# The left-over rows' output product in a forward recurrence: summed over all heads per 128 output columns, and turned by VectorE in 32x32 blocks

## The chip, the core and the metric

The kernel runs on one core of a Trainium2 chip. The metric is the device time of one execution in microseconds (us), lower is better. TensorE multiplies (PE in the profile; its weight loads, which overlap the multiplications, are PEld), VectorE (DVE), ScalarE (ACT) and GpSimd (POOL) do the rest, and SyncE (SP) issues transfers.

## What is computed

The reference is a forward and backward pass of a parallel sum: a memory-augmented recurrent attention (A) and a squared-ReLU feed-forward layer (B), with gradients of the input, the first memory and all weights. The change lies in the forward pass of A:

```python
for s in range(n_seg):                       # 64 segments of 32 rows
    xs = x[:, s * seg_len:(s + 1) * seg_len, :].copy()
    h = jnp.concatenate([mem, xs], axis=1)   # 8 memory rows, then 32 rows
    q = jnp.einsum('btd,dhe->bhte', h, Wq)   # 32 heads of 128, d = 512
    ...
    p = _softmax(scores, axis=-1)
    o = jnp.einsum('bhqk,bhke->bhqe', p, v)
    o = jnp.einsum('bhte,hed->btd', o, Wo)
    mem = o[:, :M, :].copy()                 # the next segment's memory
    outs.append(o[:, M:, :])
```

Only the first 8 rows of `o` feed the next segment. Nothing waits for the rest inside the recurrence.

## The kernel before

The kernel works in stages: layer norm and B (to some 305 us), the forward recurrence (305 to 1203), a stage that prepares the backward pass (1222 to 1455), the backward recurrence (1455 to 2415) and the weight gradients (2470 to the end). The change is in the forward recurrence.

A segment has 40 query rows. The 32 rows that are done at once (8 memory rows and 24 others) are a *step*, `fwd(s)`. The 8 left over are put aside and done later, for four segments together, as 32 rows: that is `left(b)`, for a block b of four segments. There are 64 steps and 16 blocks. The heads are laid out as 4 groups (HG, index g) of 8 (KH, index k), and TensorE is used as four column groups of 32, so that four matmuls with 32 stationary columns each run side by side, the one of group c writing PSUM partitions 32c to 32c+31 (`tile_position=(0, 32 * g)`).

The order of all work is written out by hand. `F_ORDER` (L603) has four strings, one for each step of a block (j = 0 to 3); names without a prefix are operations of the step, names with `L.` are operations of a left-over block, and a `+` or `-` behind a name moves it one round later or earlier. `play` (L581) issues the operations in that order, and every engine works through its own share in order. `ENGS` (L620) says which engine does a copy (`L.ra` and `ra` VectorE, `rb` ScalarE). The left-over block played beside block n is n - 1.

A step's chain is: K, Q and V projections (`k0mm` to `v1mm`, L392), evictions to SBUF, turns of K and Q (`k0fl` and so on, evicted by `k0Te` and so on), scores (`s0`, `s1`, L437), softmax on VectorE and ScalarE (`mx`, `sb`, `ex`, `su`, `rc`, `pm`), a turn of E on VectorE (`tu`, L450), the products with V (`w0`, `w1`, L547) and their evictions (`oa`, `ob`, to OT), the output product over all heads (`g0`, `g1`, L460), its copy to SBUF (`ra`, `rb`), four fp32 turns on TensorE (`ta`, `tb`, L469), and VectorE's sum over the four head groups, of the memory rows into X (`HT`, L482), which is the next step's input, and of the other rows into XT (`xt`).

The left-over block does the same for its 32 rows: `L.S0` to `L.W1`, evictions to OTL, and then the part that changes:

- `L.G0` and `L.G1` (`gather`, L453 to 462): the output product, one half each (p = 0, 1; in the order written, G1 comes first, in the third step, and G0 in the fourth). For each k, four matmuls, one per head group g in column group g, with 32 columns of OTL as weights and the head's whole `Wo[:, h, :]` of 512 columns moving. So PSUM's ps_RL holds four partial sums, one per head group, of 32 rows by 512 columns.
- `L.ra`: VectorE copies ps_RL (128x512 fp32) to SBUF, R4L.
- `L.ta`, `L.tb` (`turn_ops`, L464): TensorE turns R4L in four fp32 blocks of 128x128 into a further PSUM buffer, ps_sum.
- `L.xt` (`left_sums`, L473): VectorE sums the four head groups out of ps_sum, in four reductions, into the rows 0 to 7 of each segment of XT (128 x 4 x 4 x 32 fp32, two buffers).

`L.BT` in the next block's first step turns XT back to rows (`block_rows`, L485), `L.out` adds and `L.sx` stores them. PSUM buffers of the stage are four banks of one kind ("r"), shared by all of these, and the pair of bank pairs f_pp for `w`.

In the third and fourth steps the pieces stand here (L611 to L614):

```python
"tu1 oa0 ld L.G1 w1 soV- ob0 L.t2 km ob1 oa1 L.mtr g0 g1 ra L.P5 soP rb L.E5 tb ta HT",
"L.G0 k0mm xt- L.ra q0mm kl q1mm k1mm k0ev q0ev k0fl q1ev k1ev q0fl k0Te q1fl q0Te k1fl L.u2 s0 q1Te "
"L.lv+ L.lb k1Te L.t1 L.ta s1 mx0 sb0 mx1 sb1 v0mm ex0 ex1 v0ev v1mm su0 rc0 pm0 v1ev L.mst L.tb tu0 su1 "
"w0 rc1 ob0 L.P4 pm1 tu1 L.xt oa0 L.E4 w1 oa1 soV- soN- g0 ob1 g1 km rb soV ra kl+ L.S0+ tb ta L.X2 soP "
```

For the last block, 64 jobs that turn weights in place are hung behind certain operations (`done`, L924 to 929): Wo's behind `L.ra`, `L.tb` and `L.xt`.

Of the kernel before, what the change touches and what calls it, by code (L numbers as in the profile page):

```python
# [11 lines left out]
F32 = mybir.dt.float32  # L12
P = 128
# [13 lines left out]
def kernel(  # L27
# [27 lines left out]
    nc = tc.nc  # L55

    _, S, D = A_x.shape
    M = A_mem0.shape[1]
# [4 lines left out]
    L = M + SEG  # L63
# [39 lines left out]
    HG = 4  # L103
    KH = H // HG
# [79 lines left out]
    with sb("p1b", 2) as p1b, sb("p1", 1) as p1:  # L184
# [66 lines left out]
        for rb in range(NRB):  # L251
# [17 lines left out]
            for fc in range(FC):  # L269
                ps = pst([P, RB], F32, name="ps_h1")  # L270
                for dc in range(DC):
                    nc.tensor.matmul(ps[:], lhsT=W1[:, dc, fc * P:(fc + 1) * P], rhs=HT[:, dc, r0:r0 + RB],
                                     start=(dc == 0), stop=(dc == DC - 1))
                nc.scalar.activation(rT[:, fc, :], ps[:], ACT.Relu, bias=b1T[:, fc:fc + 1], scale=1.0)
                nc.vector.tensor_tensor(out=aT[:, fc, :], in0=rT[:, fc, :], in1=rT[:, fc, :], op=ALU.mult)
            for fc in range(FC):
                ps2 = pst([P, RB], F32, name="ps_ga")
                for dc in range(DC):
                    nc.tensor.matmul(ps2[:], lhsT=W2T[:, dc, fc * P:(fc + 1) * P], rhs=gT[:, dc, r0:r0 + RB],
                                     start=(dc == 0), stop=(dc == DC - 1))  # L280
# [18 lines left out]
            for rc in range(RCB):  # L299
                rr0 = r0 + rc * P  # L300
                psB = pst([P, D], F32, name="ps_B")
                for fc in range(FC):
                    nc.tensor.matmul(psB[:], lhsT=aT[:, fc, rc * P:(rc + 1) * P], rhs=W2[:, fc, :],
                                     start=(fc == 0), stop=(fc == FC - 1))
# [6 lines left out]
                for fc in range(FC):  # L311
                    nc.tensor.matmul(psG[:], lhsT=gh1T[:, fc, rc * P:(rc + 1) * P], rhs=W1T[:, fc, :],
                                     start=(fc == 0), stop=(fc == FC - 1))
# [3 lines left out]
                for srcT, dstD in ((aT, S_AN), (gh1T, S_GH1N)):  # L317
                    Nt = p1b.tile([P, F], BF16, name="Nt", tag="Nt")
                    for (f0b, nb) in GRPF8:
                        ps = pst([P, nb * P], BF16, name="ps_trf")  # L320
# [14 lines left out]
    Wo = wop.tile([P, H, D], BF16, name="Wo")  # L335
# [19 lines left out]
    with sb("fl", 2) as fl:  # L355
# [4 lines left out]
        for q, t, g, h in ALL_LEFT[:FIRST]:  # L360
            if h == 0:
                dN = fl.tile([P, GW], BF16, name="dNL", tag="dNL", bufs=6)
            ps = pst([P, 512], F32, name="ps_L")
# [36 lines left out]
    def heads_of(W):  # L400

        return lambda h: W[:, h, :]
# [50 lines left out]
    def gather(R, XT, W, h, first, last):  # L453

        for k in range(4 * h, 4 * h + 4):
            for g in range(HG):
                x, o = W(g * KH + k), R[32 * g:32 * g + 32, :]
                if len(x.shape) == 3:
                    o = o.rearrange("p (a b) -> p a b", b=P)
                nc.tensor.matmul(o, lhsT=XT(k, g), rhs=x,  # L460
                                 start=(first and k == 4 * h), stop=(last and k == 4 * h + 3),
                                 tile_position=(0, 32 * g))

    def turn_ops(o, alloc, R4, st):  # L464

        def tT(c):
            if "T" not in st:
                st["T"] = alloc("ps_sum")
            nc.tensor.transpose(st["T"][:, c * P:(c + 1) * P], R4()[:, c * P:(c + 1) * P], identF[:])  # L469
        for h in range(2):  # L470
            o["t%s" % "ab"[h]] = lambda h=h: [tT(c) for c in (2 * h, 2 * h + 1)]

    def left_sums(XT, T):  # L473

        for c in range(DC):
            nc.vector.tensor_reduce(XT[:, c], T[:, c * P:(c + 1) * P].rearrange("p (g j t) -> p j t g", g=HG, j=SPB),
                                    axis=AX.X, op=ALU.add)
# [103 lines left out]
    def play(order, n, steps, lefts, step, blk, done=None):  # L581
# [38 lines left out]
    ENGS = on_engines(  # L620
        "L.E1 L.E2 L.E4 L.oa0 L.ob0 k0ev k1ev oa0 ob0 ob1 q1Te q1ev rb v0ev v1ev",
        "L.E0 L.E3 L.E5 L.oa1 L.ob1 L.pm0 L.pm1 L.ra k0Te k1Te oa1 pm0 pm1 q0Te q0ev ra")
    with sb("fw", 1) as fw, psum("fr", 4) as fr, psum("fpp", 1) as fpp, \
# [36 lines left out]
        fo = fstack.enter_context(sb("fo", 1))  # L660
# [27 lines left out]
        def left(b):  # L688

            B_ = block(b)  # L690
            ps, st, o = {}, {}, {}
# [24 lines left out]
            for p in range(2):  # L716
                def S_(p=p):
                    ps["s%d" % p] = big("ps_scL")
                    scores(ps["s%d" % p], B_["qL"], ((B_["kM"], NL), (B_["kL"], NL)), p, maskL)
                o["S%d" % p] = S_  # L720
                soft_ops(o, p, KW, lambda p=p: ps["s%d" % p], lambda: B_["EL"], st, fo, "L", "L.")

                def tu(p=p):
                    st["ET%d" % p] = fo.tile([P, 4, 2, 32], BF16, name="ETL", tag="ETL%d" % p)
                    turn(st["ET%d" % p], B_["EL"], p)
                o["tu%d" % p] = tu

                def W_(p=p):
                    ps["w", p] = pair_of_banks()
                    outer(ps["w", p], p, ((32, 32, False, 32, B_["vM"], lambda k: st["ET%d" % p][:, k % 4, 0, :]),  # L730
                                          (32, 32, False, 32, B_["VL"], lambda k: st["ET%d" % p][:, k % 4, 1, :])))
                o["W%d" % p] = W_
                for x, n in enumerate("ab"):
                    e = "o%s%d" % (n, p)
                    o[e] = lambda p=p, x=x, e=e: ENGS["L." + e](
                        B_["OTL"][:, HALF[p], 2 * x:2 * x + 2].rearrange("p k g r -> p g k r"), two_of(ps["w", p], x, 32))

                def G_(p=p):
                    if "R" not in ps:
                        ps["R"] = big("ps_RL")  # L740
                        ps["n"] = 0
                    ps["n"] += 1
                    gather(ps["R"], lambda k, g: B_["OTL"][:, k, g, :], heads_of(Wo), p, ps["n"] == 1, ps["n"] == 2)
                o["G%d" % p] = G_

            def ra():
                st["R4"] = fo.tile([P, D], F32, name="R4L", tag="R4s")
                ENGS["L.ra"](st["R4"][:], ps["R"][:])
            o["ra"] = ra
            turn_ops(o, big, lambda: st["R4"], st)  # L750
            o["xt"] = lambda: left_sums(B_["XT"][:, :, :, 0:M], st["T"])

            def BT():
                ps["B"] = big("ps_rows")
# [3 lines left out]
            for i in range(PER):  # L758
# [3 lines left out]
                q, t, g, h = ALL_LEFT[FIRST + PER * b + i]  # L762
# [174 lines left out]
    with sb("la", 2) as la, sb("ls", 2) as ls, sb("lo", 1) as lo_, sb("wg", 2) as wg, psum("lpp", 1) as lpp, psum("lr", 4) as lr:  # L937
# [138 lines left out]
        with tc.manual_schedule():  # L1076
# [3 lines left out]
            for b in range(NB + 1):  # L1080
                for nm in LB_ORDER:
                    k = nm.rstrip("-")
# [461 lines left out]
```

## Time and profile before

| what | us |
|---|---|
| three runs | 3054.18, 3060.76, 3061.45 |
| median of the runs | 3060.76 |
| span of the profiled execution, first to last instruction | 3059.8 |
| TensorE busy in the forward recurrence (305 to 1203 us) | 830.6 of 898 |
| VectorE busy there | 577.0 |
| ScalarE busy there | 401.6 |
| TensorE idle between forward recurrence and next stage | 18.3 |

The page gives the span of the profiled execution, and no other time of it. The other times come from runs without a profile. The pieces that change, each over the whole kernel:

| operation | instructions | us each | stands at |
|---|---|---|---|
| ps_RL<-Wo,OTL, TensorE matmul 128x512 | 512 | 0.38 (four side by side) | L460 |
| loads of OTL, 128x32 | 512 | 0.10 | L460 |
| R4L<-ps_RL, VectorE copy 128x512 fp32 | 16 | 0.69 | L377 |
| ps_sum<-identF,R4L, TensorE fp32 turn 128x128 | 64 | 0.27 | L469 |
| XT<-ps_sum, VectorE reduction 128x32 <- 128x128 | 64 | 0.28 | L476 |

In the lines shown below, a time line has the start and the length in us, the engine, the line of the code, the operation, what it writes and reads, the shapes, how many were merged, and, in brackets, how long the engine had been idle before and what ended that. A matmul's length contains its way through the array, so matmuls of a stream start more densely than their lengths say. A stretch's line has its bounds and length, the busy time and number of instructions of each engine, the granted share of TensorE's clock, the DMA share and GB/s.

### The profile page before, as it was taken

How to read it: one execution, taken by the hardware profiler on the slowest of the kernel's cores; microseconds unless marked ns; L12 is line 12 of the kernel's file. 1: busy time of each engine (PE TensorE's matmuls, PEld its weight loads, DVE VectorE, ACT ScalarE, POOL GpSimd, SP SyncE). 2: the span in 40 equal slices, each digit the busy share in tenths (PEclk: the TensorE clock that was granted, in tenths of full speed). 3: DMA queues.
4: the chain of work that ended last, by engine and by line, in shares of the span. 5: the costliest groups of instructions: out<-in, count | busy, mean ns of one | idle time of the engine just before them, and what ended most of it. 6: DMA issues, size and time to landing. Idle time of an engine off the chain costs nothing. (4 is left out here: it accounts for less than half of the span.)

```text
span 3059.8 us, 109712 instructions
## 1 busy us (share of the span) xinstructions
PE 2705.4 (88%) x48600; PEld 1386.8 (45%) x48600; DVE 1319.5 (43%) x3581; ACT 994.7 (33%) x2306; POOL 658.0 (22%) x1264
## 2 busy tenths in 40 slices
PE   8997899999999886877799899998989559999998
PEld 4453444444444444446444444444444224444443
DVE  5452566666666664334345444544545201100010
ACT  2422444444444444323333333333333101111111
POOL 0000000000000000113343433434343213322222
PEclk9998999999999998999999999999999879999999
DMA  9548375766767767777577676776777899898991
GB/s 257 185 146 250 101 188 161 189 181 172 190 168 182 165 157 192 229 230 220 149 173 174 190 187 164 177 203 169 176 200 175 238 192 217 194 211 207 204 207 39
DMA packets 794559, 566.78 MB, mean 185 GB/s; under 512 B 579409, under 2 KB 681570, under 8 KB 790754
## 3 DMA queue, kind: packets, MB, share of 16 engines
q1 hardware_dynamic: 748322, 430.47, 58.8%
q0 software_dynamic: 40528, 126.53, 13.5%
q8 instruction: 381, 6.24, 0.9%
q10 hardware_dynamic: 5232, 2.75, 0.4%
q14 instruction: 96, 0.79, 0.1%
HBM read 193.61 MB, written 238.56 MB: 141 GB/s over the span
## 5 line engine op out<-in xcount | busy, mean ns | idle before, releaser
L1505 PE MATMUL ps_gw<-gn,HNc 128*128 128x512 bf16 x1920 | 416.4, 379 | 0.0
L1505 PEld LDWEIGHTS <-HNc 128*128 128x128 bf16 x1920 | 187.8, 98 | 223.9
L374 ACT CAST f_N<-ps_proj 128x512 bf16<-128x512 f32 x320 | 185.9, 581 | 243.9 <-PE ps_proj L392 223.4
L1476 ACT CAST wt<-ps_gw 128x512 bf16<-128x512 f32 x128 | 74.4, 586 | 503.5 <-PE ps_gw L1505 474.4
L392 PEld LDWEIGHTS <-X 128*32 128x32 bf16 x6144 | 153.3, 97 | 161.3 <-DVE X L482 13.9
L835 POOL COPY kM<-f_kT 128x256 bf16<-128x256 bf16 x64 | 25.6, 401 | 786.7 <-DVE f_kT L377 594.9
L1459 DVE TENSOR_TENSOR gx<-ps_rows,gb 128x512 f32<-128x512 f32 x16 | 11.1, 692 | 420.5 <-PE ps_rows L1457 418.2
L1505 PE MATMUL ps_gw<-GOc,gn 128*128 128x512 bf16 x640 | 142.2, 385 | 54.8 <-DMA GOc<-S_GM 54.8
L460 PE MATMUL ps_gR<-Wk,gk 128*32 128x512 bf16 x2048 | 146.7, 386 | 19.4 <-ACT gk L374 12.9
L392 PE MATMUL ps_proj<-Wk,X 128*32 128x512 bf16 x2048 | 135.4, 384 | 12.6 <-DVE X L482 6.9
L460 PE MATMUL ps_gR<-Wq,gq 128*32 128x512 bf16 x2048 | 141.6, 382 | 1.2 <-issue 1.2
L374 ACT CAST gk<-b_pp 128x256 bf16<-128x256 f32 x192 | 68.8, 377 | 208.3 <-PE b_pp L547 146.6
L1477 POOL DMA_DIRECT2D out_dram<-wt x128 | 69.2, 541 | 309.5 <-ACT wt L1476 309.4
L1239 POOL COPY PD<-b_P 32x320 bf16<-32x320 bf16 x256 | 114.9, 449 | 95.3 <-PE b_pp L1292 64.4
L460 PE MATMUL ps_gR<-Wv,gv 128*32 128x512 bf16 x2048 | 133.4, 379 | 0.3 <-issue 0.3
L392 PE MATMUL ps_proj<-Wo,GT 128*32 128x512 bf16 x2048 | 123.9, 384 | 7.9 <-POOL GT L1203 6.7
L392 PE MATMUL ps_proj<-Wq,X 128*32 128x512 bf16 x2048 | 128.7, 382 | 0.0
L460 PE MATMUL ps_R<-Wo,OT 128*32 128x512 bf16 x2048 | 126.4, 388 | 0.0
L469 PE MATMUL ps_sum<-identF,R 128*128 128x128 f32 x512 | 102.4, 295 | 24.6 <-ACT R L374 18.4
L392 PE MATMUL ps_proj<-Wv,X 128*32 128x512 bf16 x2048 | 124.1, 378 | 0.0
L1505 PEld LDWEIGHTS <-gn 128*128 128x128 bf16 x640 | 63.4, 99 | 132.3 <-issue 59.6
L374 ACT CAST gON<-ps_proj 128x512 bf16<-128x512 f32 x128 | 74.9, 585 | 143.2 <-PE ps_proj L392 141.5
(260 smaller groups left out, 5128.0 us busy)
## 6 DMA issues: line engine op xcount, KB each, us to landing
S_A<-f_N SPq DMA_DIRECT2D x64, 512.0 KB
out_dram<-wt POOLq DMA_DIRECT2D x142, 128.0 KB, 4.6
S_A<-f_N SPq DMA_DIRECT2D x64, 256.0 KB
S_GB<-gv SPq DMA_DIRECT2D x32, 512.0 KB
S_GB<-gq SPq DMA_DIRECT2D x32, 512.0 KB
S_GB<-gk SPq DMA_DIRECT2D x32, 512.0 KB
b_kN<-S_A POOLq DMA_DIRECT2D x63, 256.0 KB, 5.0
b_qN<-S_A POOLq DMA_DIRECT2D x63, 256.0 KB, 5.4
```

The source lines that it names most:

```text
L374: nc.scalar.copy(out, in_)
L392: nc.tensor.matmul(o, lhsT=hT[:, dc, :], rhs=x, start=(dc == 0), stop=(dc == DC - 1), tile_position=(0, 32 * g))
L460: nc.tensor.matmul(o, lhsT=XT(k, g), rhs=x, start=(first and k == 4 * h), stop=(last and k == 4 * h + 3), tile_position=(0, 32 * g))
L469: nc.tensor.transpose(st["T"][:, c * P:(c + 1) * P], R4()[:, c * P:(c + 1) * P], identF[:])
L835: o["km"] = lambda: nc.gpsimd.tensor_copy(B_["kM"][:, :, :, lc], T["kT"][:, :, :, 0:M])
L1239: nc.gpsimd.tensor_copy(PD[32 * g:32 * g + 32, g], C["P"][32 * g:32 * g + 32, :, 0:L])
L1459: nc.vector.tensor_tensor(out=gx[:], in0=ps[:], in1=gb[:], op=ALU.add)
L1476: nc.scalar.copy(wt[:], ps[:])
L1477: pdma(dst, wt[:])
L1505: nc.tensor.matmul(ps[:], lhsT=l(rc), rhs=r(rc), start=(n == 0), stop=(n == RC_ALL - 1))
```

## The change

The output product of the left-over rows is arranged anew. The new function lets each column group c make 32 of every 128 output columns, and lets all heads add up in it:

```diff
+    def gather_columns(R, XT, W, h, first, last):
+        for k in range(4 * h, 4 * h + 4):
+            for g in range(HG):
+                x = W(g * KH + k)
+                for c in range(HG):
+                    nc.tensor.matmul(R[32 * c:32 * c + 32, 0:P].rearrange("p (a b) -> p a b", b=32), lhsT=XT(k, g), rhs=x[:, :, 32 * c:32 * c + 32],
+                                     start=(first and k == 4 * h and g == 0), stop=(last and k == 4 * h + 3 and g == HG - 1),
+                                     tile_position=(0, 32 * c))
...
-                    gather(ps["R"], lambda k, g: B_["OTL"][:, k, g, :], heads_of(Wo), p, ps["n"] == 1, ps["n"] == 2)
+                    gather_columns(ps["R"], lambda k, g: B_["OTL"][:, k, g, :],
+                                   lambda h: Wo[:, h, :].rearrange("p (a b) -> p a b", b=P), p, ps["n"] == 1, ps["n"] == 2)
...
-            def ra():
-                st["R4"] = fo.tile([P, D], F32, name="R4L", tag="R4s")
-                ENGS["L.ra"](st["R4"][:], ps["R"][:])
-            o["ra"] = ra
-            turn_ops(o, big, lambda: st["R4"], st)
-            o["xt"] = lambda: left_sums(B_["XT"][:, :, :, 0:M], st["T"])
+            o["ra"] = lambda: nc.vector.transpose(B_["XT"][:, :, :, 0:M], ps["R"][:, 0:P])
+            o["ta"] = o["tb"] = o["xt"] = lambda: None
```

For each head (k, g) there are now four matmuls with the same 32 weight columns, one in each column group, each with 128 moving columns: 4 runs of 32 columns, 128 apart. Column group c thus holds output columns 32c to 32c+31 of each of the four 128-blocks, for the 32 rows, already summed over all 32 heads, in 128 columns of PSUM. VectorE's block turn, which turns every 32x32 block in place, makes of this exactly the layout of XT, so one instruction from PSUM straight into XT stands where the copy, the four turns and the four reductions were. It stands at the place of `L.ra`; the places of `L.ta`, `L.tb` and `L.xt` are empty. `F_ORDER` is as it was, and so are the weight turns of the last block, which hang on the names. The steps' own `gather` and turns, and the backward pass, are not touched.

## Prediction

> **What bounds the kernel now.** I read the page's head first, to see which engine is full, then the busy times by stretch, to get a steady unit of time, then the order of time inside that unit.
>
> ```profile
> span 3059.8 us, 109712 instructions
> ...
> PE 2705.4 (88%) x48600; PEld 1386.8 (45%) x48600; DVE 1319.5 (43%) x3581; ACT 994.7 (33%) x2306; POOL 658.0 (22%) x1264
> ```
>
> TensorE is busy for 88% of the whole span, which invites the reading that any TensorE work taken away is time won. The change touches only the forward recurrence (305 to 1203 us), where 64 steps follow each other through the memory rows: a step's result, reduced by VectorE into X, is the input of the next step's first projection. I cut that stretch at the starts of this reduction (X<-ps_sum). Columns: stretch, its length, then the busy time and count of each engine, the granted clock, the DMA share.
>
> ```profile
> 345.03:358.25 13.22, 11.21 (x280) 5.94 (x281) 6.94 (x20) 5.37 (x12) 0.80 (x2) 1.00 0.24 83
> ...
> 698.62:711.84 13.22, 12.44 (x286) 6.38 (x281) 8.20 (x24) 5.96 (x13) 0.80 (x2) 1.00 0.75 179
> ...
> 725.35:739.03 13.68, 13.56 (x304) 6.89 (x301) 8.36 (x27) 5.85 (x13) 0.80 (x2) 1.00 0.51 166
> ```
>
> The first line is the fourth step of block 0, which has no left-over work beside it; the second is the second step of block 7; the third is the fourth step of block 7, where nearly all that the change touches is played (L.G0, L.ra, L.ta, L.tb, L.xt). So all left-over work in such a step costs 13.68 - 13.22 = 0.46 us, although it is more than 2 us of TensorE and 2 us of VectorE. A step is a chain of latencies, and left-over work mostly lies in its gaps. There are 15 such steps (blocks 1 to 15 each play the block before). Inside one:
>
> ```profile
> 398.74 1.05 PE L460 MATMUL ps_RL<-Wo,OTL 128*32 128x512 bf16 x16
> 398.85 0.29 DVE L482 TENSOR_REDUCE X<-ps_sum 128x32 bf16<-128x128 f32 x1
> ...
> 399.61 1.04 PE L392 MATMUL ps_proj<-Wk,X 128*32 128x512 bf16 x16
> 399.91 0.69 DVE L377 COPY R4L<-ps_RL 128x512 f32<-128x512 f32 x1 [0.30 <-PE ps_RL L460]
> ...
> 401.56 0.69 DVE L377 CAST f_N<-ps_proj 128x512 bf16<-128x512 f32 x1 [0.97 <-DMA S_VTM<-vTM]
> ...
> 404.75 0.44 PE L469 MATMUL ps_sum<-identF,R4L 128*128 128x128 f32 x2
> ...
> 407.06 0.45 DVE L450 STREAM_TRANSPOSE ET<-E 128x256 bf16<-128x256 bf16 x1
> ...
> 407.13 0.44 PE L469 MATMUL ps_sum<-identF,R4L 128*128 128x128 f32 x2
> ...
> 407.56 0.20 PE L547 MATMUL f_pp<-ET,f_N 32*128 32x32 bf16 x4
> ...
> 408.68 0.85 DVE L476 TENSOR_REDUCE XT<-ps_sum 128x32 f32<-128x128 f32 x4
> ```
>
> Here one sees where each piece lies. X is ready at 399.14, but the K projection starts at 399.61, because G0 holds TensorE until then; in the step before, X's reduction ended at 385.70 and the projection began at 385.76. G0 therefore delays the chain by about 0.40 us, nearly the whole 0.46. The other four pieces lie beside waits.
>
> **The change, part by part.**
>
> *Gather, 16 matmuls of 512 columns become 64 of 128, per half.* Four matmuls on four column groups run side by side: in ps_RL the starts come in fours, and the fours are 216 ns apart (16 matmuls in 1.05 us: 3 x 216, and about 0.39 for the last). After, the same stream is 16 waves of 128 columns. No row shows column groups at 128 columns. The nearest are the bf16 turns of 128 columns on the whole array, 56 ns apart (ps_wt at 1192: eight in 0.62), and column groups with 32 columns:
>
> ```profile
> 411.26 0.20 PE L437 MATMUL ps_scL<-kM,qL 128*32 128x32 bf16 x4
> 411.30 0.19 PE L437 MATMUL ps_scL<-kL,qL 128*32 128x32 bf16 x4
> 411.32 0.19 PE L437 MATMUL ps_scL<-kM,qL 128*32 128x32 bf16 x4
> 411.35 0.19 PE L437 MATMUL ps_scL<-kL,qL 128*32 128x32 bf16 x4
> ```
>
> A wave of four there takes 25 ns with four weight loads of just the new shape (128x32), so loads and issue fit into 56 ns. I take 56: 16 x 56 = 896 against 4 x 216 = 864, so +0.032 us a half. Ends: below, 4 x 216 / 16 = 54 ns, no cost; above, no packing at all, 4 x 56 = 224 ns a wave, +2.72 us a half. Between, if a wave had to wait for its loads (97 ns each in the groups, L460 PEld), 153 ns, +1.58. I keep 56 because the 25 ns row is nearest in form. The strided moving operand (32 of every 128 columns) I cost at nothing: L1292 reads runs of 8 and its 64 columns leave room for the next matmul after 0.03 us.
>
> G0's excess is on the chain: 15 x 0.032 = +0.5 us. G1's is covered: in the step before, G1 starts at 393.90, would let the next matmul go at 394.77, and that one waits for VectorE's turn of E (394.35 + 0.45) and starts at 394.95. It has 0.14 us to spare; beyond that it costs in full.
>
> *L.ra, copy of 0.69 us becomes one block turn.* The turn of 128 fp32 elements from PSUM is not in the trace. Nearest: the reduction of as many fp32 from PSUM, 0.28; the bf16 turn of 256 elements, 0.45; the copy itself, 0.69. I take 0.3. It decides nothing: VectorE next works at 401.56, when the Q projection's product comes, so anything up to 1.6 us from 399.91 is hidden.
>
> *L.ta and L.tb, four fp32 turns, gone.* L.ta holds TensorE for 0.27 us (404.75 to 405.02) ahead of the second half's scores. Their reader, VectorE's maximum, starts at 405.54, behind VectorE's own subtraction (405.25 + 0.32), so at most 0.05 us is won; compared with the step before, the same reading starts 0.04 later relative to the first scores. That is 15 x 0.04 = -0.6. The V projection behind it gets 0.27 earlier, but its products wait for E's turn until 407.51. L.tb lies in just that wait: the outer products start at 407.56, 0.05 after the turn's end, with or without it. Worth 0; if the softmax on VectorE were quicker by 0.1 us, it would be worth that.
>
> *L.xt, four reductions (0.85 us), gone.* They stand between E's second turn and one eviction of OT. That eviction starts at 409.45; the outer products it reads end at 409.28, so it comes up to 0.1 us earlier. Its reader is the second half of the gather, which runs with the first half in one unbroken stretch from 409.20. Worth 0.
>
> *No DMA is added or moved; no queue of SP or POOL is passed.* One PSUM buffer less is taken per block, XT is written some 9 us earlier into a tile with two buffers. After the last step, G0, turn and the Wo turns run from 1190 to 1201; then TensorE stands idle from 1203.2 to 1221.5 until l_gON's eviction, held up by the loads of kM behind SP's OCl turns. Those hang on OTL, not on the gather. Worth 0; without that cover, 0.69 - 0.3 + 0.66 + 0.85 = 1.9 us once.
>
> *Sum.* +0.5 - 0.6 = -0.1 us on a span of 3059.8. The runs' median, 3060.76, is 0.96 above this span, which I take for what lies around it: 3060.7. The three runs themselves spread over 7.3 us.
>
> **A rule weighed.** The Trainium skill, "TensorE: Matmul & The Clock Gate", section "Back-to-back issue gap", gives about 81 ns a matmul for a sustained stream of load and matmul pairs at 128 columns, and its section "The mechanism" lets loads overlap running matmuls only where the row groups differ, which they don't here. The 25 ns waves above, whose row groups are also all alike, speak against the second. By 81 ns a wave a half would take 1.30 us, G0 +0.43 and G1 +0.29, and the sum would be 15 x 0.72 = 10.9 us, an estimate from that page: 3071.6.
>
> **The rivals.**
>
> *Slower: waves longer than 56 ns.* Place: G0 ahead of the K projection, price one for one, 15 times; G1 less 0.14. It decides (over 0.3%, 9.2 us, about what a measurement of this kernel can tell from no change) from 15 x (2x - 0.14) = 9.2, x = 0.38 us a half, 78 ns a wave. At 153 ns: 15 x (1.58 + 1.44) = 45 us, 3106. At 224: 15 x (2.72 + 2.58) = 80 us, 3140. For it: no row has 128 columns on column groups, and a half now issues 128 instructions where it issued 32. Against: the 25 ns waves; and longer bursts of small pairs (L547 at 2403) go on at 33 ns per four pairs when the queue's stock is used up.
>
> *Faster: the relief counts.* If the fourth step fell to 13.22, 15 x 0.46 = 6.9 us, 3053.9. More than that only if work off the chain in my reading is on it: all of it, 0.54 of TensorE and 1.54 - 0.3 of VectorE, would be 15 x 1.78 = 27 us, 3034. For it: TensorE is busy for 13.56 of 13.68 us there. Against: block 0's step without left-over work is 13.22, and G0 alone, which stays, takes 0.40 of the 0.46.
>
> *It does not do what it says:* the block turn from PSUM is slow, over 1.6 us. Then Q's eviction is late by the rest; a 2 us turn costs 15 x 0.4 = 6 us, 3067.
>
> **How the numbers follow.** Forecast, within some 4 us of 3060.7: 0.58. Relief in part, 3053 to 3057: 0.13; relief beyond 9.2 us: 0.07. Mildly longer waves or a slow turn, 3065 to 3069: 0.09; waves over 78 ns: 0.13. So faster 0.07, same 0.80, slower 0.13. The range 3053 to 3069 takes in the three middle cases, 0.80.
>
> **What would show it.** Right: ps_RL<-Wo,OTL as 2048 matmuls of 128 columns in waves 56 ns apart; the K projection still 0.47 us behind X's reduction in the fourth step; R4L gone; 16 block turns XT<-ps_RL of about 0.3 us; steps of 13.22 and 13.68 us unchanged. Wrong: the fourth step shorter than 13.5 (relief), or G0 and G1 well over 1.1 us each and the third and fourth steps longer by the excess.

## The result: 0.5% slower, and the profile after

Five runs of the changed kernel took 3069.94 to 3084.55 us, median 3075.59; five of the kernel before took 3054.18 to 3063.62, median 3060.76. The ratio is 1.0049, 95% interval 1.0032 to 1.0066: slower, by more than the 0.3% that can be told from no change, and beyond the range. The profiled execution has a span of 3069.2 us, against 3059.8.

The head of the page after:

```profile
span 3069.2 us, 112428 instructions
...
PE 2692.6 (88%) x49923; PEld 1399.5 (46%) x50072; DVE 1301.6 (42%) x3517; ACT 993.0 (32%) x2306; POOL 658.1 (21%) x1264
```

VectorE's busy time is 17.9 us less than before, and the span is 9.4 longer. (TensorE's 12.8 less says little: 149 matmul records are missing in this trace, and in second profiles TensorE is busy for 2709.7 us in both kernels.) Less work in more time means that something waits. First the two operations of the change, in the tile view of ps_RL (durations are minimum, median and maximum in ns, then first and last start in us):

```profile
L470 PE MATMUL ps_RL<-Wo,OTL x2048: 216/219/231, 395.2 to 1201.6; 128*32 128x128 bf16 x187
L757 DVE STREAM_TRANSPOSE XT<-ps_RL x16: 316/317/319, 401.6 to 1201.9; 128x128 f32<-128x128 f32 x16
```

There are 2048 matmuls and 16 block turns of 0.317 us, as foreseen. Next the time lines of the fourth step of block 8, the counterpart of the lines shown of before:

```profile
785.63 1.08 PE L470 MATMUL ps_RL<-Wo,OTL 128*32 128x128 bf16 x64
785.74 0.29 DVE L492 TENSOR_REDUCE X<-ps_sum 128x32 bf16<-128x128 f32 x1
...
786.54 1.04 PE L392 MATMUL ps_proj<-Wk,X 128*32 128x512 bf16 x16
786.76 0.32 DVE L757 STREAM_TRANSPOSE XT<-ps_RL 128x128 f32<-128x128 f32 x1 [0.27 <-PE ps_RL L470]
```

L.G0 takes 1.08 us against 1.05, and the K projection starts 0.51 us behind the end of X's reduction (786.54 against 786.03), 0.04 later than before. (1.08 - 0.22) / 15 makes waves 57 ns apart, and the step behaves as worked out. So the stretches, with the columns as in the prediction: first the fourth step of block 0, then the second step of block 7, the fourth step of block 8, and the *third* steps of blocks 4 and 8.

```profile
346.35:359.57 13.22, 11.21 (x281) 5.96 (x281) 6.94 (x21) 5.38 (x12) 0.80 (x2) 1.00 0.23 82
...
704.72:717.94 13.22, 12.23 (x284) 6.38 (x282) 8.20 (x23) 5.96 (x13) 0.80 (x2) 1.00 0.76 166
...
785.74:799.40 13.66, 12.91 (x347) 7.03 (x344) 7.26 (x23) 5.87 (x13) 0.80 (x2) 1.00 0.55 164
...
550.55:565.98 15.43, 12.71 (x321) 6.85 (x326) 8.28 (x23) 5.44 (x12) 0.80 (x2) 1.00 0.95 216
...
772.30:785.74 13.44, 12.32 (x321) 6.85 (x326) 8.19 (x22) 5.46 (x12) 0.80 (x2) 1.00 0.99 234
```

The first three are 13.22, 13.22 and 13.66 us, as before or 0.02 below. The third steps, which the prediction called covered, are what moved: the same instructions (x321, x326, x12) in 15.43 us in one block and 13.44 in another. Before, these two took

```profile
548.50:562.18 13.68, 12.48 (x270) 6.29 (x274) 8.28 (x22) 5.44 (x12) 0.80 (x2) 1.00 0.90 232
766.16:779.60 13.44, 12.48 (x270) 6.28 (x274) 8.19 (x22) 5.46 (x12) 0.80 (x2) 1.00 0.91 232
```

Over the 16 third steps the sum goes from 215.4 to 222.9 us, and the forward recurrence, from the first to the last reduction into X, from 842.4 to 854.6 (the rest of the program is 2.8 us shorter in this profile, so the spans differ by 9.4). The rest of the 12.2 us lies in five first and second steps that take 14.7 to 15.1 us, and these have another cause. One of them, and then the one such step that the kernel before has, and a first step that has the same instructions and not that length:

```profile
1144.54:1159.25 14.71, 12.43 (x278) 6.01 (x273) 8.20 (x23) 5.47 (x12) 0.80 (x2) 0.88 0.78 185
```

```profile
1118.76:1134.14 15.38, 13.05 (x331) 7.10 (x334) 10.75 (x32) 6.50 (x16) 0.80 (x2) 0.89 0.47 109
1064.44:1078.43 13.99, 11.94 (x331) 6.45 (x334) 10.75 (x33) 6.51 (x16) 0.80 (x2) 1.00 0.40 86
```

The granted clock is 0.88 and 0.89 there, not 1.00: the clock record has 0.5 for 3.41 us in each, and the step's output product runs in fours that are mostly 400 to 415 ns apart, where they are 205 to 217 apart otherwise. Every first or second step of 14.7 us or more, in all profiles of all kernels here, has such a stretch, one to five of them in a profile. Why the clock falls just there was not tried.

Inside the third step of block 4, TensorE's time lines are:

```profile
559.30 1.08 PE L470 MATMUL ps_RL<-Wo,OTL 128*32 128x128 bf16 x64
...
560.64 0.83 PE L460 MATMUL ps_R<-Wo,OT 128*32 128x512 bf16 x11
...
562.84 0.97 PEld L460 LDWEIGHTS <-OT 128*32 128x32 bf16 x21 [1.86 <-issue]
562.84 1.47 PE L460 MATMUL ps_R<-Wo,OT 128*32 128x512 bf16 x21 [1.37 <-issue]
```

The step's own output product (`g0`, `g1`), one unbroken stretch of 32 matmuls before, stops after 11 and goes on 1.7 us later. The twelfth belongs to `g0` like the eleven, and reads the half of OT that ScalarE had cast from 559.46 on. What the profile names is "issue": nothing that it shows. In the view of TensorE's waits in the forward recurrence (in all, times, longest) that line is new:

```profile
PE ps_R L460 <- issue: 3.6, 4, 1.4
```

Before, all of TensorE's matmul waits on issue there sum to 0.3 us, one wait. (The view also has 22 waits of ps_L on issue, 3.9 us. They come from 58 matmul records of ps_L that are missing in this trace; a second profile, with all records, has one such wait.)

**A trail.** The page's queue table has a kind of traffic that the prediction did not read. Before, then after (packets, MB, share):

```profile
q8 instruction: 381, 6.24, 0.9%
```

```profile
q8 instruction: 392, 6.42, 0.9%
```

6.24 MB in 381 packets is 16384 bytes each. Before, TensorE has 97535 records: 97200 matmuls and loads, and 335 of its sequencer, nearly all semaphore instructions. 97535 / 381 = 256.0, so a packet is 256 instructions of TensorE. Its instructions come by DMA while it works. In the hole above, the trace has such a packet from 560.374 to 561.393 us; the last matmul before the hole starts at 561.09, the next one at 562.84. The densest 2.5 us of a third step hold 196 of TensorE's records before and 292 after: `w0` (64), L.G1 (128, before 32), `w1` (64), and the start of `g0`. 292 is more than a packet.

### The profile page after: what moved, and what is told of

It is laid out like the page before. It is cut to its first block, busy times and chain, and to the rows that moved or that the text cites. A ratio compares the mean times of both kernels' runs of the same rounds, so it can differ in the third digit from the quotient of the medians.

```text
span 3069.2 us, 112428 instructions
## 1 busy us (share of the span) xinstructions
PE 2692.6 (88%) x49923; PEld 1399.5 (46%) x50072; DVE 1301.6 (42%) x3517; ACT 993.0 (32%) x2306; POOL 658.1 (21%) x1264
## 5 line engine op out<-in xcount | busy, mean ns | idle before, releaser
L1512 PEld LDWEIGHTS <-HNc 128*128 128x128 bf16 x1920 | 187.9, 98 | 223.8
L392 PEld LDWEIGHTS <-X 128*32 128x32 bf16 x6144 | 152.1, 97 | 158.4 <-DVE X L492 14.1
## 6 DMA issues: line engine op xcount, KB each, us to landing
S_A<-f_N SPq DMA_DIRECT2D x64, 256.0 KB
b_kN<-S_A POOLq DMA_DIRECT2D x63, 256.0 KB, 4.9
b_qN<-S_A POOLq DMA_DIRECT2D x63, 256.0 KB, 5.0
```

What stands on the lines that cost most here:

```text
L392: nc.tensor.matmul(o, lhsT=hT[:, dc, :], rhs=x, start=(dc == 0), stop=(dc == DC - 1), tile_position=(0, 32 * g))
L1512: nc.tensor.matmul(ps[:], lhsT=l(rc), rhs=r(rc), start=(n == 0), stop=(n == RC_ALL - 1))
```

## The experiments

Four theories were on trial. **A, supply:** the added instructions outrun the packets. **B, waves:** the new matmuls, or their loads, are longer than 56 ns in places. **C, relief or buffers:** with the copy, turns and reductions gone, buffers come free earlier, and transfers collide. **D, number:** each added instruction costs, wherever it stands.

The whole times of the runs below hold a disturbance. On their chips the untouched backward recurrence (first ps_sc from gOT to last reduction into GT) took 935 to 957 us, against 930 in the first profile, and differed by 14 us between two profiles of the same kernel; the medians of before are 3070.8 to 3073.4 there. Ratios go by runs of before taken beside the run; the mechanism is read from the forward recurrence. That is one profile for each run: two profiles of the kernel before have 842.4 and 842.0, two of the changed kernel 854.6 and 851.3, and each step with a halved clock (below 1.00 in the lines above) adds some 1.1 to 1.7 us to it.

| run | ratio, 95% | forward recurrence | third steps, sum | fourth, median | densest 2.5 us from the third on |
|---|---|---|---|---|---|
| before | 1 | 842.4 | 215.4 | 13.68 | 196 |
| changed kernel | 1.0049 (1.0032 to 1.0066) | 854.6 | 222.9 | 13.65 | 292 |
| e1, both halves cut | 1.0047 (1.0031 to 1.0064) | 855.2 | 226.5 | 13.71 | 292 |
| e2, block turn alone | 1.0006 (0.9987 to 1.0025) | 842.4 | 215.3 | 13.62 | 196 |
| e3, L.G1 elsewhere | 1.0023 (1.0006 to 1.0040) | 848.5 | 219.4 | 13.65 | 247 |
| e4, and L.G0 in two | 1.0024 (1.0007 to 1.0041) | 841.5 | 217.7 | 13.37 | 216 |
| e5, L.G1 cut | 1.0021 (1.0001 to 1.0042) | 853.0 | 225.9 | 13.67 | 292 |
| e6, L.G0 cut | 0.9995 (0.9976 to 1.0014) | 841.8 | 215.1 | 13.71 | 196 |
| e7, both cut in 256 | 1.0012 (0.9993 to 1.0031) | 844.3 | 216.0 | 13.69 | 228 |
| a0, changed again | one run | 851.3 | 223.0 | 13.65 | 292 |
| e8, mtr later | 1.0060 (1.0044 to 1.0077) | 851.9 | 223.8 | 13.65 | 292 |
| e9, four pieces | 1.0034 (1.0009 to 1.0059) | 845.1 | 221.2 | 13.37 | 228 |
| e10, and mtr later | 1.0021 (1.0000 to 1.0043) | 847.5 | 221.5 | 13.36 | 228 |
| e11, good offset | 1.0024 (1.0002 to 1.0046) | 848.4 | 217.0 | 13.65 | 292 |
| e12, bad offset | 1.0113 (1.0086 to 1.0140) | 877.6 | 245.6 | 13.65 | 279 |
| e13, four old places | 1.0010 (0.9986 to 1.0034) | 846.8 | 215.5 | 13.70 | 228 |
| e14, and good offset | 1.0031 (1.0011 to 1.0050) | 848.3 | 217.2 | 13.83 | 228 |
| e15, e4 with an offset | 0.9981 (0.9959 to 1.0002) | 838.0 | 215.1 | 13.37 | 216 |

### The number alone, and the turn alone

`e1_count_both` is the kernel before, with each matmul of 512 columns cut into four of 128; the copy, turns and sums stay.

```diff
+    def gather_split(R, XT, W, h, first, last, N=P):
+        for k in range(4 * h, 4 * h + 4):
+            for c in range(0, D, N):
+                for g in range(HG):
+                    nc.tensor.matmul(R[32 * g:32 * g + 32, c:c + N], lhsT=XT(k, g), rhs=W(g * KH + k)[:, c:c + N],
...
-                    gather(ps["R"], ...
+                    gather_split(ps["R"], ...
```

> The kernel before, with each of the 512-column matmuls of both left-over halves cut into four of 128 columns; the copy, the fp32 turns and the reductions stay. So it has the changed kernel's number of TensorE instructions and nothing else of it. Theory A (instruction supply: the 128 instructions of G1 stand between w0 and w1, together more than one 16 KB instruction packet within 2.5 us, and TensorE runs dry when the packet comes late): slower like the change, ratio 1.003 to 1.007, the excess in the third steps, which become erratic (13.4 to 15.4 us), and ps_R streams with holes of 0.5 to 1.9 us. Theory B (the 128-column waves themselves are longer): G0 and G1 over 1.2 us each, third and fourth steps longer by the same amount in every block. Theory C (the relief of VectorE or the new PSUM order disturbs the transfers): ratio 1.000 within 0.001, since neither is changed here.

`e2_turn_only` is its counterpart: the old gather, and the block turn of ps_RL's first 128 columns in the place of copy, turns and sums.

> The kernel before with the old gather, but the block turn from PSUM in place of copy, fp32 turns and reductions. It turns the first 128 columns only, and the sum over the four head groups is left out, so the left-over rows are not the reference's. Theory A: no loss, ratio 0.998 to 1.001; the fourth steps 13.65 us, the third 13.43 without spread. Theory C: slower like the change, ratio 1.003 to 1.007, with spread third steps. Theory B: as theory A.

e1 gives the whole loss (ratio 1.0047, third steps 13.4 to 15.7 us, sum +11), and e2 none of it: no third step moves, and the fourth is 0.06 us shorter. C falls with this pair, because all that could be relieved is gone in e2 and all of it stays in e1.

`e5_count_G1` and `e6_count_G0` cut one half each, and `e7_count_256` both halves in pieces of 256 columns:

```diff
+                    gather_split(ps["R"], ..., N=P if p == 1 else D)      # e5; p == 0 in e6; N=2 * P in e7
```

> The kernel before with 128-column matmuls in G1 alone (between w0 and w1 in the third step); G0, copy, turns and reductions as before. Theory A (instruction supply runs dry in a burst): the third steps as long and as erratic as with both halves cut, 8 to 13 us more over the forward recurrence, fourth steps 13.68; ratio 1.003 to 1.006. Rival D (more TensorE instructions cost everywhere, in proportion to their number): half of the loss with both halves cut, 1.002.

> The same with G0 alone (ahead of the K projection in the fourth step, whose neighbours are long matmuls). Theory A: third steps 13.43 without spread, fourth steps 13.71, forward recurrence within 2 us of 842; ratio 0.998 to 1.002. Rival D: as much as with G1 alone, 1.002, forward recurrence 848.

> The kernel before with both halves cut into matmuls of 256 columns: 64 instructions a half, the burst around G1 some 230 in 2.5 us, fewer than the 256 of a packet. Theory A: a third of the loss or less, 0 to 4 us in the third steps. Rival D: a third of 12 us, 4 us, spread over third and fourth steps.

The same 96 instructions more cost 10.6 us around L.G1, between `w0` and `w1`, and nothing around L.G0, ahead of projections of 512 columns. D falls, and B too, since the matmuls and loads are alike. (e5's whole time, 1.0021, is below what A gave for it and just what D gave; e6, where D had 1.002 as well, is what speaks against D.) At 228 instructions in 2.5 us (e7) one third step of 16 is late by over 0.3 us.

### Another place, and other pieces

`e3_swap` exchanges L.G1 with L.P5 (four matmuls of 512 columns), so that L.G1 stands behind `ra` and no longer before `w1`. `e4_split` also cuts L.G0 in two halves of 64 instructions each, 32 matmuls and 32 loads (L.Gb at L.tb's old place, the block turn at L.xt's).

```diff
-        "tu1 oa0 ld L.G1 w1 soV- ob0 L.t2 km ob1 oa1 L.mtr g0 g1 ra L.P5 soP ...
+        "tu1 oa0 ld L.P5 w1 soV- ob0 L.t2 km ob1 oa1 L.mtr g0 g1 ra L.G1 soP ...
```

> The changed kernel with L.G1 and L.P5 exchanged in the third step: G1 behind g1, the four large matmuls of P5 between w0 and w1. Theory A: the burst falls to below 200 instructions in 2.5 us, the third steps go back to some 13.4 us without spread, ratio 0.998 to 1.001 to the kernel before. Theory B: no change against the changed kernel, 1.005, since G1 costs the same there. Theory C: likewise 1.005.

> As the exchange, and besides G0 is cut in two halves of 64 instructions: one stays ahead of the K projection, where TensorE has 0.47 us before X is ready, the other takes the place of the old L.tb, where it waits for the turn of E; the block turn goes to the old place of L.xt. Theory A, with the reading that G0 alone holds up the fourth step by 0.4 us: the fourth step falls from 13.65 to 13.25 us, 15 times, so 6 us below the exchange: ratio 0.996 to 0.999. If ps_RL, held 9 us longer, takes a PSUM bank from the projections, the fourth step stays at 13.6 or grows. Theories B and C: 1.003 to 1.005.

e3 gives back half: most third steps are at 13.43, but three are at 14.0 to 15.2 (13.44 before, but for block 4's 13.68), and the ratio is 1.0023, outside what A gave. So half of the loss goes with the old place; at the new one L.G1 and L.G0 follow each other closely, up to 247 records in 2.5 us across the end of the step, and now the holes (0.6 to 2.0 us) stand in L.G1 and behind it. e4's fourth step falls to 13.37, because half of L.G0 no longer stands ahead of the K projection. Its whole time does not show that; the 841.5 us of its forward recurrence do.

> The kernel before once more, for a second profile of it beside the next three. All theories: third steps 13.43 us with little spread; forward recurrence from the first to the last X reduction 842 us. It shows how far the stages that the change doesn't touch (backward recurrence 930 us in the first profile) differ from run to run; if by 10 us or more, totals of single runs decide nothing and the forward recurrence is what is compared.

The kernel before, profiled again: forward recurrence 842.0 against 842.4, but backward 944.4 against 930.4. That is why the forward recurrence is the measure.

> The changed kernel once more, as it is, for a second profile of it on the chip of the experiments. Instruction supply: the forward recurrence, first to last reduction into X, is 849 to 858 us long again (854.6 in the first profile, 842.4 and 842.0 in two of the kernel before), by third steps of 13.4 to 16 us, not the same ones as before. Rival, an accident of one execution: below 845 us.

The changed kernel, profiled again: 851.3 us, in the range. But the end of that sentence was wrong, and this was the most useful miss of the study. The late third steps *are* the same ones: block 4 has 15.43 and 15.37 us, block 5 14.77 and 14.72, block 6 14.56 and 14.59, block 8 13.44 twice. A stray transfer would not repeat itself so. Something that is fixed in the program does.

`e8_mtr` moves the DMA transpose of vM from the third step (ahead of `g0`) to the fourth, as the third has a DMA share of 0.95 to 0.99.

> The changed kernel, with the DMA transpose of vM (L.mtr) issued in the fourth step, behind q0mm, and not in the third, ahead of g0. If the packets of instructions come late because that transpose fills the DMA engines just there (DMA share 0.96 to 0.99 in the third step), the third steps fall from a sum of some 226 us to below 220 and the forward recurrence from 854.6 to below 849 us, and holes may come up in the fourth step in their place. If the number of instructions within one packet's time is enough by itself, the third steps stay erratic, 13.4 to 16 us with a sum of 223 to 230, and the forward recurrence stays at 851 to 857 us.

The third steps stay as they were (223.8): that transpose is not what decides. Their DMA share is still 0.71 to 1.07 in blocks 1 to 14, so the rest of the traffic is not tested by this. `e9_quarters` cuts both halves into two pieces (64, 64, 64, 64 instructions per block for 128, 128; a piece is 32 matmuls and 32 loads, not 64 matmuls), `e10_quarters_mtr` also moves the transpose.

> The changed kernel, with both gathers cut in two pieces of 64 matmuls: L.G1's first half where L.G1 was, its second behind ra of the third step, L.G0's first half where L.G0 was, its second in the middle of the fourth step where L.tb was, and the block turn where L.xt was. No place takes more than 32 matmuls and loads more than the kernel before had there. Instruction supply: the densest 2.5 us of the third step hold about 228 instructions, as with the 256-column cut, whose third steps summed to 216.0 us against 215.4; so third steps of 13.4 us with at most two outliers, fourth steps of 13.4 (13.37 in the cut of L.G0 alone), forward recurrence 837 to 841 us, some 2 to 5 us below the kernel before. Rival, any added instruction near L.G1 costs: third steps sum to 219 or more, forward recurrence 842 or more.

> The four pieces of 64 matmuls again, and the DMA transpose of vM in the fourth step. If that transpose is what makes packets late, the last outliers of the third steps go and the forward recurrence is 1 to 3 us shorter than with the four pieces alone; if not, the two agree within 1 us, or the fourth step takes the transpose's place and is 0.1 us longer.

e9 missed: fourth steps 13.37 as expected, but most third steps 13.81, 0.38 us longer. I had put the second piece of L.G1 behind `ra` in addition to L.P5, and take it that together they are more than `ra` and `rb` cover. Beyond that four steps are late. e10 missed too: it is 2.4 us longer than e9, and its third steps are no better.

### The place in the packet

Count all of TensorE's records from the program's start, its sequencer's included, and note for each third step the place of `w0`'s first record modulo 256. In a0 a block advances by 2546 records, 14 short of 10 packets, so that this place creeps from block to block. Excess of the third step over 13.43 us, sorted by place:

```
a0:  27 .60 |  73 .01   87 .18   97 .00  101 .00  115 .01 | 129 .72  143 1.16  157 1.29  159 1.01  171 1.94 | 185 .51  199 .34  213 .06  221 .32
e5:   9 .34  11 .63  39 .00 |  61 .02  63 .00  83 .00  111 .00  113 .00 | 145 .43  163 3.85  165 3.66 | 189 .39  213 .93  215 .46  217 .34
```

Two kernels with different gathers and different blocks, and much the same curve: nothing from 61 to 115 but for 0.18 once, the worst at 143 to 171. (Block 4's excess, at 171 and at 163, holds 0.25 that it has before the change too, and e5's 3.85 and 3.66 hold a stretch of halved clock each.) To show that this place decides, I changed it and nothing else. `e11_pad_good` and `e12_pad_bad` are the changed kernel with small matmuls ahead of the second step's `w0`, where TensorE waits for ET:

```diff
                     ps["w", p] = pair_of_banks()
+                    if p == 0 and j == 1:
+                        for i in range([39, 39, 7, 7, 7, 7, 7, 7, 7, 7, 7, 7, 23, 31, 31, 31][s // 4]):   # e12: 53, 54, 7, ...
+                            g = i % 4
+                            nc.tensor.matmul(ps["w", p][g // 2][:, g % 2, 0:32], lhsT=ident[32 * g:32 * g + 32, 0:P],
+                                             rhs=ident[32 * g:32 * g + 32, 0:32], start=True, stop=True, ...)
```

> The changed kernel plus small matmuls that compute nothing (32x128 weights, 32 columns, overwritten by w0's own), put ahead of the second step's w0, where TensorE waits for ET: 78 before the first L.G1, then 7 per block, 23 and 31 in the last four. Counting TensorE's matmul and load records from the program's start, the third step's w0 then begins at about the same place modulo 256 in every block, 113. In four profiles with L.G1 cut, third steps that began at places 97 to 115 took 13.43 us seven times in eight. If packets of 256 instructions are what decides, all third steps take 13.4 us (sum 215 to 217), and the forward recurrence is 842 to 846 us long, though more matmuls are issued than in the changed kernel (854.6, 851.3). Rival: what makes holes lies in the block (its transfers, its buffers) and not in the place; then blocks 4, 5, 6 and 14 stay at 14.4 to 15.4 us, and the forward recurrence at 850 to 857.

> The same, with 107 small matmuls ahead of the first L.G1 where the other has 78, so 58 instructions more in all: the third step's w0 begins at place 171 in every block, where two profiles showed 15.4 and 15.7 us. Packets of 256: every third step from the second block on takes 15.2 to 15.8 us, the sum is 240 to 251, the forward recurrence 866 to 878 us, some 25 us more than with the other offset. Rival, the place doesn't matter: the two runs agree within 4 us.

The two differ by 29 small matmuls, near the start, out of 50 thousand. Third steps of blocks 4 and 8, first with the good offset (place 113), then with the bad one (place 171):

```profile
552.33:566.01 13.68, 12.48 (x322) 6.84 (x326) 8.28 (x22) 5.45 (x12) 0.80 (x2) 1.00 1.01 215
770.59:784.02 13.43, 12.48 (x322) 6.84 (x326) 8.19 (x22) 5.47 (x12) 0.81 (x2) 1.00 1.04 211
```

```profile
555.23:571.21 15.98, 12.88 (x322) 6.86 (x326) 8.27 (x23) 5.44 (x12) 0.80 (x2) 1.00 1.04 207
781.36:796.53 15.17, 12.88 (x322) 6.86 (x326) 8.17 (x23) 5.47 (x12) 0.80 (x2) 1.00 1.11 220
```

Block 4 took 15.4 us in the changed kernel and is at 13.68 again, as before the change; block 8 was unharmed and is now at 15.17. All 15 third steps of e12 with an L.G1 are late, by 1.1 to 4.1 us (14.6 to 17.5 us, a wider spread than the 15.2 to 15.8 expected; the three over 17 us have a stretch of halved clock behind the hole). The forward recurrences are 848.4 and 877.6 us, the medians of the runs, taken side by side, 3078.5 and 3105.1. The waits of TensorE on issue in e12's forward recurrence, which e11 doesn't have on ps_R:

```profile
PE ps_R L460 <- issue: 20.2, 15, 2.1
```

and its block 8, where the stretch again breaks after the eleventh matmul:

```profile
789.84 1.08 PE L470 MATMUL ps_RL<-Wo,OTL 128*32 128x128 bf16 x64
...
791.19 0.83 PE L460 MATMUL ps_R<-Wo,OT 128*32 128x512 bf16 x11
793.39 1.47 PE L460 MATMUL ps_R<-Wo,OT 128*32 128x512 bf16 x21 [1.37 <-issue]
```

Last, the holes themselves. In e12, a0, e1 and e5, all 27 holes of over 0.7 us inside the ps_R stretch stand at the same record modulo 256, number 193: 15, 5, 5 and 2 of them. That is the edge of a packet, and the packet that lands just before TensorE goes on is each time the one that is due by the count. The holes of e3 and e4, in L.G1 and just behind it, stand at 193 as well. In the kernel before, e6, e7 and e15 no gap at this record in the forward recurrence is over 0.5 us. In e12, TensorE goes on 1.2 to 1.5 us after the packet has landed, and 2.2 to 3.0 us after its transfer began. A packet's transfer takes 1.0 us (median in the forward recurrence).

Two further counts show why a dense stretch runs dry. In all traces with complete records, no packet's transfer starts more than 297 records ahead of the packet's first instruction, and no first instruction runs sooner than 2.15 us after that start. So TensorE has little more than one packet ahead of it at most. An estimate from these numbers: at 292 records in 2.5 us, 2.15 us are 251 records, and most transfers start with a smaller lead than that (median some 200); at the 196 of before they are 169.

What remained wrong in e11's expectation: 848.4 us, not 842 to 846. The sum of the third steps came (217.0), but three of them are late by 0.4 to 1.0 us at the good place, ahead of `w0` and not at a packet's edge. Two second steps (13.9 and 14.1 us in the last blocks, with 31 small matmuls) have holes of 0.9 and 1.1 us at record 193, one at the start has the halved clock, and several fourth steps were late.

### A version from this

> The changed kernel with its 128 matmuls per block in four pieces of 32 matmuls to a half's quarter, so 64 instructions and loads each at a place where the kernel before had left-over work: L.G1's place, L.G0's place, L.ta's place and L.tb's place, and the block turn at L.xt's place. Third steps lose half of L.G1 (1.08 to some 0.54 us) and take 13.0 to 13.4 us with a few outliers of up to 1 us, as a cut in 256 columns has the same density, 228 instructions in 2.5 us; fourth steps 13.35 to 13.45. Forward recurrence 832 to 839 us against 842, ratio 0.997 to 0.999. Rival, any added instruction near L.G1 costs: third steps as in the four pieces before, 13.8 us, and 843 us or more.

> The four places again, with the small matmuls of the good offset (78, then 7 per block). If what outliers are left come from the place in the packet, the third and first steps' outliers go, and the forward recurrence is 0 to 3 us shorter than with the four places alone, less some 1 us for the small matmuls. If not, the two differ by the small matmuls alone, 0 to 2 us longer.

`e13_slots` puts the four pieces at the places of L.G1, L.G0, L.ta and L.tb. Its third steps are free of holes (215.5), but they did not get shorter by the half of L.G1 that left, and the fourth steps are at 13.70: it seems that a piece at L.ta's place takes back what half an L.G0 gave. The expectation of 832 to 839 us fell (846.8); four first and second steps are late by 0.3 to 1.6 us each as well, three of them with the halved clock. e14 is 1.5 us longer than e13 (848.3), so the good offset won nothing here.

> The changed kernel with L.G1 behind ra of the third step and L.G0 in two halves of 64 matmuls (the cut of L.G0 run before: forward recurrence 841.5 us, with outliers in the third and fourth steps only at places 73 to 171), and small matmuls ahead of the second step's w0, 7 per block and 23 to 31 in the last four, so that the third step's w0 begins at place 213 in every block, where that kernel had no outlier. Packets of 256: third steps 13.44 us throughout (sum 215 to 216 against 217.7), fourth steps 13.37 (sum 200 to 201 against 201.7), forward recurrence 837.5 to 841 us, some 1 to 4.5 us below the kernel before; in the whole time that is at most 0.15%, ratio 0.998 to 1.001. Rival, the outliers lie in blocks 4, 5, 7 and 14 and not in the place: third steps as they were, 841 to 843 us.

`e15_split_pad` is e4 with 7 small matmuls per block, 23 to 31 in the last four, and none before, so that `w0` starts at place 213, where e4 had no late step. Third and fourth steps of block 8:

```profile
763.17:776.61 13.44, 12.41 (x322) 6.96 (x326) 8.11 (x23) 5.46 (x12) 0.80 (x2) 1.00 0.87 231
776.61:789.98 13.37, 13.08 (x348) 7.12 (x343) 7.19 (x22) 5.95 (x13) 0.80 (x2) 1.00 0.76 202
```

All third steps are as before the change (215.1), the fourth steps of blocks 1 to 14 at 13.36 to 13.37, and the forward recurrence is 838.0 us, as expected, 4.0 below the 842.0 of the kernel before. The ratio, 0.9981 (0.9959 to 1.0002), agrees with that and cannot be told from no change.

## Why the prediction was wrong, point by point

- *Gather, waves of 56 ns: right.* They are 57, and e6, which has them ahead of the K projection in the old kernel, has a fourth step 0.03 us longer, the 0.032 reckoned. The figure of 81 ns that the Trainium skill gives ("TensorE: Matmul & The Clock Gate", section "Back-to-back issue gap") is not what this stream shows: a wave of four such pairs takes 57.
- *L.ra, 0.3 us, hidden: right* (0.317 us). So were *L.ta and L.tb, -0.04 us*: with G0's +0.03 the fourth step went from 13.681 to 13.652, and e2, which has the turn alone, has -0.06. R4L and its turns are gone, and nothing else came off the chain.
- *G1's excess is covered: the step that failed.* Its cover of 0.14 us held for its duration. But the term that mattered was not a duration. I had the count in hand ("a half now issues 128 instructions where it issued 32"), used it for the rival of longer waves, and put it aside with the sentence that "loads and issue fit into 56 ns" and that longer bursts go on "when the queue's stock is used up". That argument takes a rate from a place of 25 or 33 ns per four pairs and treats supply as a rate. It is a stock, delivered in packets of 256, 2.2 to 3.0 us from the start of a transfer to its use where it ran out; what counts is how many instructions run in that time, and where the edge of a packet falls. In place of 0 the runs show +7.5 and +7.6 us in the third steps, in two profiles. First and second steps add 5.4 us in the first profile and 2.0 in the second. The long ones among them have the halved clock, which the kernel before has too (15.38 us once); whether the change brings it on more often is not shown.
- *The rival "slower"* had the right side and the wrong mechanism: no wave got longer, L.G0 and L.G1 are 1.08 us, and its price one for one at G0 is not seen. Most holes fall into `g0` and `g1`, which the change does not touch. The two other rivals did not come about.
- *No DMA is added: wrong in a way that the page showed.* q8 carries 11 packets more. It is 0.9% of the DMA time, so I passed over it; its weight is in its lateness, not in its share.

Open points: why TensorE goes on only 1.2 to 1.5 us after a packet has landed, and what starts a packet's transfer (in e12's late ones it starts 0 to 115 records ahead of the edge, while half of all lead by some 200 or more), no run here tells. Nor was it tried what brings on the halved clock in a few first and second steps of nearly all kernels. The Trainium skill, "Trainium Architecture — The Big Picture", section "The software stack", lets instruction streams be moved to the engines when a program is loaded; the 381 packets within this execution show that TensorE's, here, come while it runs.

## What to carry to other kernels

Count instructions as well as time: where a change multiplies small matmuls, count TensorE's matmuls and loads in the densest 2.5 us, and compare with the 256 of a packet of the "instruction" queue; up to 196 no third step was late by over 0.3 us here, at 216 to 228 none to four of 16, at 279 to 292 three to all 15, by the place. A wait on "issue" in the middle of an untouched stretch, in the same places in each profile but not in each repetition of a loop, points to supply; check whether the holes stand at one record number modulo 256. Put added instructions next to long matmuls (e6: free) and not between short ones (e5: 10.6 us). And look at the granted clock of a step that is late without a hole: here it was 0.5 for 3.41 us.

## What the runs showed of the hardware that was not expected

- The time of a kernel can depend on where its instructions fall in packets: 58 instructions more near the start (e12 against e11) cost 29.2 us in the forward recurrence, 3.4%, with the same work in every later block.
- A third step with a hole shows only part of it as a wait: in e12 the waits on ps_R sum to 20.2 us, the holes between records to 25.8 us, and the third steps to 28.6 us more than in e11.
- VectorE's block turn of 128x128 fp32 elements straight from PSUM takes 0.317 us, against 0.69 for the copy of four times as much, and 0.28 for the reduction of as many.
